# Linear attention and a gated causal unit on one core: nine tokens of a head per partition instead of four and a tail

## The chip, the core and the metric

The kernel runs on one core of a Trainium2 chip. The core has TensorE (PE), VectorE (DVE), ScalarE (ACT), GpSimd (POOL) and SyncE (SP); each takes its instructions in order from a list of its own and waits on semaphores for the others. Matrix products land in PSUM, which here is one tile `PS` of 128 partitions and 8 banks of 512 floats. Loads, stores and the transposing copies are DMAs, issued by SP, POOL or ACT.

The metric is the device time of one execution, in microseconds.

## The reference

There are 8 batches, 8 heads, 576 tokens, and 64 values per head. The first half is a linear attention with exponential features, the second a gate made by a causal convolution of five taps:

```python
def phi(x):
    proj = x @ w_phi                                  # 64 -> 128
    proj = proj - max(abs(proj), axis=-1)
    return concatenate([exp(proj), exp(-proj)])       # 256 features
kv = einsum('bhsf,bhsd->bhfd', phi(k), v)
z  = sum(phi(k), axis=2)
x  = (phi(q) @ kv) / (phi(q) @ z + 1e-06)             # heads side by side: 8 x 576 x 512
gate = 1 / (1 + exp(-sum_k conv_w[k] * x[s - 4 + k])) # zeros ahead of token 0
out  = (gate * (x @ w_val)) @ w_out
```

Inputs and output are float32; the kernel's matmuls take bf16.

## The kernel before, in words

A **unit** is two heads (a pair, `hp`) of one batch over the first 512 tokens. Each partition holds four consecutive tokens of a head, so a token is named by partition and place `j` (0 to 3). The last 64 tokens of two batches make a **tail** unit: 36 units in all, 32 mains and 4 tails.

Steps of a main unit, by the names in the list:

- `T`, `Tc` (L331, L224 or L222): eight transposes of 128x128 put k and q into one PSUM bank; one copy takes them to SBUF. Row half 0 then holds one place, row half 1 the next.
- `PK`, `PQA` (L342): the projections with tokens on the partitions, 64-row matmuls into two banks each. `mKa`, `mK`, `mQa`, `mQ` (L356): their largest absolute values, on DVE.
- `K0` to `K3` (L388): the exponentials of k, plus and minus, per bank, on ACT. The maximum of k is not subtracted; `E` (L382, two small exponentials) makes the factors and `V` (L408, L412, on POOL) multiplies them into v, with the factor itself as a 65th column.
- `PQ` (L466) projects q with features on the partitions; `SH` (L476) subtracts its maximum by a matmul with a negative identity; `Qa`, `Q` (L484) are its four exponentials.
- `KV` (L445, L450): the sums over tokens, 4 results of four matmuls over 128 partitions and one from the tail (`VZ`, which has zeros where the other batch sits). `KVM` copies the result to SBUF as `KVS`.
- `NUM` (L509, tails L523), `XN` (L534, L536: reciprocal and product on DVE), `XP` (L545, L548): numerators, division, and a transposing DMA on SP into `XT` (mains) or `XH` (tails), channels on the partitions.

For a batch: `GA` (L604) does the five taps by 64x64 diagonal tiles, two blocks of 32 matmuls; `TH` (L612) a tanh of the halved sum (weights are halved, so that 0.5 * (tanh + 1) is the sigmoid); `VA` (L617) the value product; `GV` (L633) their product; `OUT` (L642), `OE` (L649, L651: times 0.5) and `ST` the output. Tails have `GAt` (L673, L681), `THt`, `GVt`, `OUTt` (L704), `OEt`, `STt` of their own. `HL` copies the four tokens in front of a tail.

Loads `LD` go through POOL's queue, those of the first v and the first pair of k through SP. The order of all the work is the string `ORDER`, written out in advance: one token a step, with the PSUM bank behind `@` and the engine behind `:`. Each engine executes its own instructions in this order; nothing is moved at run time.

Of the kernel before, what the change touches and what calls it, by code (L numbers as in the profile page):

```python
# [10 lines left out]
ALU = mybir.AluOpType  # L11
# [9 lines left out]
SM = 512  # L21
ST = S - SM
E1 = D + 1
PL = 144
TL = 80
NG = B // 2
NU = 9 * NG


# [3 lines left out]
LD7 LD6 CK0 CQ0 T1@1 LD2 ND0:A W20 Tc1:D PK1@2,5 mKa1 PQA1@6,1 K01 mK1 mQa1 mQ1 T0@0 LD0 Tc0:A  # L33
PQ1@3,4 PK0@7,6 K11 K21 mKa0 T2@0 E1 Tc2:D K31 K00 SH1 Qa1 LD1 PK2@1,0 mK0 mKa2 LD3 mK2 PQA2@3,5
mQa2 ZV0:P LD8 K20 mQ2 T3@2 E0 Tc3:D PQA0@3,5 mQa0 mQ0 K02 K10 K30 E2 K22 PK3@7,6 mKa3 PQA3@2,5
LD4 mQa3 Q1 LD9 PQ2@3,4 SH2 LD10 mK3 K32 K12 T4@0 Tc4:D PK4@1,0 K03 Qa2 mQ3 V0:P K23 V1:P KV1@3 Q2
LD5 V2:P mKa4 K33 K04 KVM1:D NUM1@4 PQ3@6,3 SH3 mK4 XN1 LD11 K13 KV2@2 K24 LD31 PQA4@7,4 KVM2:D E3
mQa4 K14 mQ4 PQ0@1,5 K34 SH0 LD30 Qa3 Qa0 NUM2@6 PQ4@2,0 T5@4 T6@1 Q3 SH4 Q0 XN2 Qa4 E4 Tc5:D
Tc6:D PK5@7,6 mKa5 K05 PQA5@3,1 PK6@2,5 mQa5 Q4 LD13 K15 mK5 LD12 V3:P K25 KV3@3 mQ5 V4:P mKa6 K06
LC0 K35 KVM3:D E5 V5:P LD32 LD39 PQ5@0,1 TP0@7 mK6 Vb0:P NUM3@3 CW0 XP1 XN3 K16 XP2 T7@7 Tc7:D K26  # L40
SH5 Qa5 PQA6@6,2 mQa6 PK7@3,7 mKa7 KV4@4 PQA7@6,0 mQ6 mQa7 XP3 K36 T8@5 Tc8:D mK7 PQ6@2,6 Q5
KVM4:A SH6 K07 NUM4@4 mQ7 XN4 E6 PK8@0,1 K17 mKa8 Qa6 K27 T9@2 Tc9:D Q6 XP4 PQA8@3,5 V6:P PQ7@4,6
SH7 mQa8 LD15 mK8 K08 K37 PQA9@2,3 mQ8 mQa9 KV5@7 KVM5:D mQ9 T10@5 Tc10:D K18 PQ8@0,2 SH8 Qa7
PK9@4,7 mKa9 T11@3 E7 V7:P Q7 PK10@5,6 Tc11:D K28 mKa10 LD14 DG0:P Qa8 K38 KV6@3 Q8 K09 NUM5@0 mK9
KVM6:D NUM6@2 XN5 K010 mK10 KV7@0 K29 K110 XN6 K19 KVM7:D T12@5 PK11@1,4 mKa11 K210 HL0:P Tc12:D
XP6 LD16 K39 GA0@2 K310 mK11 K011 NUM7@6 VAa1@0 LD40 XN7 E8 VAb1 TH0 GV1 V8:P PK12@2,5 PQA10@3,6
K111 PQ9@1,7 SH9 VAa2@0 K211 mQa10 mKa12 LD19 VAa0@3 mK12 E9 LD17 K311 Qa9 VAb0 mQ10 KV8@4 KVM8:D
VAb2 GV0 PQA11@1,6 K012 V9:P Q9 mQa11 K212 PQ10@4,7 SH10 mQ11 K112 T13@3 Tc13:D NUM8@1 XN8 E10
K312 Qa10 Q10 GA1@5 TH1 PK13@3,4 mKa13 NUM0@1 V10:P KV10@7 XN0 KVM10:D XP5 XP0 XP8 E11 E12 K013
mK13 VAa3@5 GV2 PQ11@6,1 SH11 K113 Qa11 V11:P VAb3 GV3 LD18 K213 NUM10@2 XN10 T14@0 Tc14:D Q11  # L50
KV11@7 XP7 PQA12@5,6 K313 GA2@2 E13 TH2 PK14@0,1 mQa12 mQ12 PQA14@4,5 OUT1@6 OE1:A KVM11:D
PQA13@7,2 mQa14 V12:P V13:P mKa14 LD34 K014 mQ14 mQa13 K114 PQ12@3,4 SH12 XP10 KV12@6 mQ13 T15@5
Qa12 KVM12:A Tc15:D OUT2@7 Q12 mK14 K214 NUM11@2 E14 PQ13@0,6 SH13 Qa13 XN11 XP11 NUM12@4 OE2:D
XN12 T16@2 VAa6@3 PK15@7,0 mKa15 GA3@4 mK15 K314 V14:P VAa4@1 Q13 Tc16:D VAb4 K015 TH3 PQA15@6,2
GV4 K215 K315 PQ14@5,4 SH14 mQa15 K115 mQ15 VAa5@1 VAb5 PK16@0,6 Qa14 VAb6 Q14 KV13@7 GV5 mKa16
mK16 Vb9:P K016 VAa7@2 T17@1 GV6 E15 V15:P Tc17:D LD33 KVM13:A KV14@5 LD22 HL1:P NUM13@3 K116 K216
PQ15@0,7 KVM14:A VAb7 XN13 K316 SH15 GV7 PK17@1,3 mKa17 Qa15 K017 Q15 K117 LD35 mK17 XP13
PQA16@5,6 mQa16 OUT3@4 XP12 K217 OE3:D mQ16 OUT0@2 OUT5@0 K317 OE5:A E16 V16:P OE0:D NUM14@4 T18@1
XN14 Tc18:D GAt0@6 THt0 ST1 GVt0 E17 PQ16@2,3 PK18@1,0 SH16 Qa16 mKa18 Q16 T19@4 Tc19:D GA4@5 TH4
PQA18@7,2 mK18 mQa18 E18 KV15@4 KVM15:D K018 LD38 K118 V17:P K218 OUT6@3 mQ18 OE6:D PQA17@7,6 K318  # L60
mQa17 mQ17 LD20 GA5@4 TH5 PK19@2,3 mKa19 PQ18@1,7 SH18 K019 KV16@0 mK19 Qa18 KVM16:D K119 E19
NUM15@5 VAa9@4 VAb9 LD21 V19:P K219 ST3 XN15 XP15 GV9 NUM16@0 XN16 Q18 LD24 T20@2 VAa8@5 XP16 VAb8
K319 T21@6 PQA19@4,0 PQ17@1,7 Tc20:D PK20@2,3 Tc21:A SH17 GV8 Qa17 mQa19 VAa10@5 VAb10 mKa20 K020
XP14 KV17@6 V18:P mQ19 Q17 GV10 VAa11@0 PK21@1,4 KVM17:D K120 mK20 mKa21 mK21 K220 VAb11 GV11
NUM17@5 XN17 OUTt0@2 K021 K221 LD26 KV19@7 OUT7@0 K320 OEt0:D OE7:D K121 T22@3 PQA20@5,2 mQa20
PQ19@1,6 mQ20 SH19 KVM19:A K321 Tc22:A HL2:A PK22@0,5 mKa22 NUM9@3 XN9 XP9 Qa19 OUT4@7 Q19 K022
# [12 lines left out]
XN25 HL4:A OUTt1@2 Q26 K028 K128 KVM26:D OUT14@7 OE14:D XP25 K228 PQA27@3,4 mQa27 mQ27 GA8@0 TH8
VAa16@7 VAb16 K328 OEt1:A NUM26@4 XN26 T29@3 Tc29:A NUM18@0 XN18 XP18 E28 OUT12@6 V28:P PK29@3,2  # L80
GV16 OE12:A PQ27@5,4 mKa29 PQA28@0,1 mQa28 mQ28 K029 SH27 Qa27 GA9@6 TH9 T30@0 ST11 VAa18@1 mK29
VAb18 Tc30:D PK30@0,5 GV18 V27:P OUT15@6 VAa17@7 VAb17 mKa30 Q27 OE15:D mK30 K129 E29 PQA29@4,6
V29:P mQa29 GV17 mQ29 PQ28@1,3 K229 K030 K130 SH28 T31@0 Tc31:D K230 VAa19@4 VAb19 Qa28 KV28@7 ST9
XP26 K329 PQA30@6,1 PQ29@2,0 SH29 GV19 mQa30 mQ30 Q28 KVM28:A K330 NUM28@3 XN28 PQ30@7,6 Qa29 E30
V30:P PK31@5,1 mKa31 SH30 PQA31@4,3 Q29 Qa30 mQa31 mK31 E31 mQ31 KV29@2 V31:P K031 K231 T32@0
OUT17@4 Tc32:D K131 OUT16@7 Q30 PK32@0,3 KVM29:D OE17:D KV30@2 mKa32 K331 OE16:A NUM29@4 KVM30:D
K032 T33@6 XP28 mK32 XN29 XP29 GA10@1 LD29 K132 Tc33:D PQA32@4,5 K232 K332 E32 PQ31@7,0 mQa32
HL5:P TH10 mQ32 OUT19@6 OE19:A NUM30@3 XN30 XP30 KV31@5 KVM31:A SH31 Qa31 Q31 PQA33@1,6 PK33@2,3
ST15 mKa33 mQa33 mQ33 GA11@4 VAa20@7 TH11 VAb20 VAa22@1 mK33 V32:P VAb22 T34@6 PQ32@4,5 K033 SH32
E33 GV22 Tc34:D NUM31@0 VAa21@6 VAb21 GV20 K133 XN31 V33:P PK34@2,7 K233 K333 mKa34 Qa32 Q32 mK34  # L90
# [10 lines left out]
"""


class _U:
    pass

@with_exitstack
def kernel(  # L110
# [11 lines left out]
    nc = tc.nc  # L122
    ctx.enter_context(nc.allow_low_precision("bf16 operands of the matmuls"))

    const = ctx.enter_context(tc.tile_pool(name="const", bufs=1))
    loadp = ctx.enter_context(tc.tile_pool(name="loadp", bufs=3))
    loadv = ctx.enter_context(tc.tile_pool(name="loadv", bufs=3))
    tailp = ctx.enter_context(tc.tile_pool(name="tailp", bufs=2))
# [635 lines left out]
```

## Time and profile before

| | |
|---|---|
| median of three runs | 234.17 us (233.95 to 235.0) |
| span of the profiled execution, first to last instruction | 232.5 us |
| its own time | not given apart from its span; the three runs stand 1.5 to 2.5 us above it |
| busy: PE, DVE, ACT, POOL | 205.8, 184.2, 188.6, 125.4 us |
| mean granted TensorE clock | 0.972 |
| DMA | 30.90 MB in 62002 packets |

Matmuls are pipelined: the time a row gives for one is its latency, and a block's length is the distance between the starts of two blocks. Engines are called busy when any of their instructions runs. The clock column gives the share of full speed that TensorE was granted. In the chain of waits each piece starts where what released it ended.

### The profile page before, as it was taken

The page shows a single profiled execution, that of the slowest core. Times are in us where ns is not written, and L with a number is a line of the kernel's source. Part 1 is how long each engine was busy: PE and PEld are TensorE (multiplying, and loading weights), DVE is VectorE, ACT ScalarE, POOL GpSimd, SP SyncE. Part 2 cuts the span into 40 slices and gives each one's busy share as a digit, 9 for nine tenths or more (in the row PEclk, how much of TensorE's full clock was granted, in tenths as well). Part 3 has the DMA queues.
Part 4 walks back from the last instruction along what each step waited for, and adds up shares of the span by engine and source line. Part 5 has one row for each costly group of instructions (what it writes and reads, how often), then busy time and mean ns, then how long its engine had stood idle before and what let it go on. Part 6 is the DMA issues. An engine that isn't in the chain of part 4 may idle for free.

```text
span 232.5 us, 8372 instructions
## 1 busy us (share of the span) xinstructions
PE 205.8 (89%) x3497; PEld 139.5 (60%) x3516; DVE 184.2 (79%) x335; ACT 188.6 (81%) x419; POOL 125.4 (54%) x142
## 2 busy tenths in 40 slices
PE   1286797888999989899999999999899999999991
PEld 1264675666666746567666766766476667564550
DVE  5559669999989979699999879897799788554451
ACT  3189869999997988599999979998899999934251
POOL 8909935999979437774919751564526241100000
PEclk9998579999999999999999999999999999999997
DMA  8997995979999942999994992499903928126195
GB/s 151 246 198 97 106 180 80 92 101 178 129 194 128 139 32 32 129 257 177 128 114 68 180 186 92 39 115 126 214 6 37 169 77 259 38 52 200 27 355 185
DMA packets 62002, 30.90 MB, mean 133 GB/s; under 512 B 33420, under 2 KB 59148, under 8 KB 61964
## 3 DMA queue, kind: packets, MB, share of 16 engines
q0 software_dynamic: 36144, 14.29, 58.2%
q1 hardware_dynamic: 25468, 15.78, 33.6%
q8 instruction: 27, 0.44, 0.8%
q10 hardware_dynamic: 352, 0.30, 0.4%
q14 instruction: 11, 0.09, 0.2%
HBM read 30.48 MB, written 9.44 MB: 172 GB/s over the span
## 4 chain that ended last, share of the span: by engine, by line
PE 69%; ACT 11%; DMA 9%; DVE 5%; issue 3%; SPq 1%; POOL 1%; POOLq 0%; DVEq 0%; ACTq 0%
PE PS L617 11%; PE PS L642 10%; PE PS L342 7%; PE PS L604 7%; PE PS L476 7%; PE PS L445 6%; PE PS L331 6%; DMA XT<-XN 6%; PE PS L509 5%; ACT QTIL L484 5%; ACT KTIL L388 3%; DMA kT<-in_k_dram 3%; PE PS L466 3%; PE PS L681 2%; DVE MQ L356 2%
## 5 line engine op out<-in xcount | busy, mean ns | idle before, releaser
L408 POOL TENSOR_TENSOR VT<-vN,E 128x1024 bf16<-128x1024 bf16 x27 | 51.5, 1907 | 60.4 <-issue 34.2
L388 ACT ACTIVATE KTIL<-PS 128x512 bf16<-128x512 f32 x128 | 76.7, 666 | 5.3 <-DVE MK L356 5.1
L484 ACT ACTIVATE QTIL<-PS 128x512 bf16<-128x512 f32 x128 | 71.0, 666 | 2.5 <-PE PS L476 1.1
L356 DVE TENSOR_REDUCE MK<-PS 128x4 f32<-128x512 f32 x72 | 47.9, 683 | 7.5 <-PE PS L342 7.2
L356 DVE TENSOR_REDUCE MQ<-PS 128x4 bf16<-128x512 f32 x72 | 47.4, 683 | 1.3 <-PE PS L342 1.2
L342 PE MATMUL PS<-W,T 64*128 64x128 bf16 x576 | 29.6, 227 | 5.8 <-DVE T L224 1.9
L617 PE MATMUL PS<-XT,WVAL 128*128 128x512 bf16 x128 | 33.8, 380 | 0.3 <-DMA XT<-XN 0.3
L342 PEld LDWEIGHTS <-T 64*128 64x128 bf16 x576 | 18.3, 98 | 21.8 <-issue 11.9
L642 PE MATMUL PS<-WOUT,GV 128*128 128x512 bf16 x111 | 29.9, 380 | 1.2 <-issue 0.5
L633 DVE SCALAR_TENSOR_TENSOR GV<-GATE,PS 128x512 bf16<-128x512 bf16 x32 | 21.6, 681 | 5.9 <-ACT GATE L612 3.1
L445 PE MATMUL PS<-VT,KTIL 128*128 128x65 bf16 x512 | 25.4, 198 | 0.8 <-DVE T L224 0.6
L536 DVE TENSOR_TENSOR XN<-PS,RCP 128x512 bf16<-128x512 f32 x36 | 24.9, 691 | 1.2
L445 PEld LDWEIGHTS <-KTIL 128*128 128x128 bf16 x512 | 22.8, 100 | 3.7 <-DVE T L224 0.8
L476 PE MATMUL PS<-nident,MQ 128*128 128x128 bf16 x288 | 23.9, 229 | 0.5 <-issue 0.5
L612 ACT ACTIVATE GATE<-PS 128x1024 bf16<-128x1024 f32 x16 | 16.7, 1044 | 8.8 <-PE PS L604 8.7
L476 PEld LDWEIGHTS <-MQ 128*128 128x128 bf16 x288 | 17.6, 102 | 9.5 <-issue 8.8
L224 DVE COPY T<-PS 128x1024 bf16<-128x1024 bf16 x31 | 21.1, 684 | 2.7 <-PE PS L331 2.3
L509 PEld LDWEIGHTS <-QTIL 128*128 128x128 bf16 x512 | 19.3, 99 | 5.5 <-DVE KVS L224 1.1
L509 PE MATMUL PS<-KVS,QTIL 128*128 128x65 bf16 x512 | 21.4, 196 | 1.3 <-DVE KVS L224 0.8
L450 PE MATMUL PS<-VZ,KTt 128*128 128x65 bf16 x128 | 21.9, 196 | 0.0
L604 PE MATMUL PS<-XT,DIAG 64*64 64x384 bf16 (+3 forms) x512 | 20.6, 299 | 1.0 <-issue 0.8
L642 PEld LDWEIGHTS <-GV 128*128 128x128 bf16 x128 | 11.3, 98 | 12.4 <-issue 0.6
(73 smaller groups left out, 304.1 us busy)
## 6 DMA issues: line engine op xcount, KB each, us to landing
out_dram<-OS SPq DMA_DIRECT2D x14, 512.0 KB, 3.8
kN<-in_k_dram POOLq DMA_DIRECT2D x7, 512.0 KB, 9.0
qN<-in_q_dram POOLq DMA_DIRECT2D x7, 512.0 KB, 8.4
vN<-in_v_dram POOLq DMA_DIRECT2D x7, 512.0 KB, 6.9
vF<-in_v_dram SPq DMA_DIRECT2D x2, 512.0 KB, 7.6
out_dram<-OSt SPq DMA_DIRECT2D x8, 128.0 KB, 2.4
out_dram<-OS SPq DMA_DIRECT2D x4, 256.0 KB, 2.9
qT<-in_q_dram POOLq DMA_DIRECT2D x8, 64.0 KB, 5.2
```

Source lines behind the costliest of these rows:

```text
L342: nc.tensor.matmul(PS[:, bank[rg], blk * P:(blk + 1) * P], u.T[r, i, blk, :], W2[r, :], start=True, stop=True,)
L356: nc.vector.tensor_reduce(dst, PS[:, bank, :].rearrange("p (b f) -> p b f", f=F), AX.X, ALU.max, apply_absolute_value=True,)
L388: nc.scalar.activation(u.KT[:, ft, rg, :, :].rearrange("p b f -> p (b f)"), PS[:, u.PK[rg], :], AF.Exp, scale=1.0 if ft == 0 else -1.0,)
L408: eng.tensor_tensor(dst[:, :, :, 0:D], x.unsqueeze(1).to_broadcast([n, 2, 8, D]), e.unsqueeze(3).to_broadcast([n, 2, 8, D]), ALU.mult,)
L445: nc.tensor.matmul(o, u.KT[:, ft, rg, h2 * 2 + j2, :], u.VT[:, ft, (h2 * 2 + j2) * 2 + rg, :], start=(c == 0), stop=False,)
L476: nc.tensor.matmul(PS[:, u.PQ[rg], blk * P:(blk + 1) * P], u.MQ[:, rg, blk:blk + 1].to_broadcast([P, P]), nident[:, :], start=False, stop= ...
L484: nc.scalar.activation(u.QT[:, ft, rg, :, :].rearrange("p b t -> p (b t)"), PS[:, u.PQ[rg], :], AF.Exp, scale=1.0 if ft == 0 else -1.0,)
L509: nc.tensor.matmul(ps[:, j2, x * E1:(x + 1) * E1], u.QT[:, ft, rg, h2 * 2 + j2, :], u.KVS[:, (ft * 2 + h2) * E1:(ft * 2 + h2 + 1) * E1], s ...
L536: nc.vector.tensor_tensor(u.XN[:, :, :, :], nv[:, :, :, 0:D], RCP[:, :, :].unsqueeze(3).to_broadcast([P, 2, 4, D]), ALU.mult,)
L604: nc.tensor.matmul(ps[c, par, j0 * P:j1 * P], DIAG[r, dt, 4 - dl, :], mv, start=(i == 0), stop=(i == len(parts) - 1), skip_group_check=True,)
L617: nc.tensor.matmul(PS[:, m.val[jt], :], WVAL[:, dt, jt * P:(jt + 1) * P], XTs[m.b % 2][:, dt, :, 16:PL], start=(dt == 0), stop=(dt == 3),)
L642: nc.tensor.matmul(PS[:, bank[0], :], m.GV[:, jt, j * P:(j + 1) * P], WOUT[:, jt, :], start=(jt == 0), stop=(jt == 3),)
```

## The change

Each partition now holds nine consecutive tokens of a head: 64 partitions per head, two heads to a tile of 128, tokens `9r + j`. Every batch is on its own. A main unit (32 of them) has the places 0 to 7 of a head pair. Place 8 of all eight heads of a batch is a **head group** `h` (8 of them), which takes the part of the tails, with steps `hT`, `hPK`, `hPA`, `hSH`, `hKp`, `hV`, `hNUM`, `hXP`, `hGA`, `hVA`, `hOUT` and so on.

- Loads are whole tensors of a batch, 2304 contiguous bytes per partition and head pair; there are no tail loads.
- `T` transposes each head's 64 partitions apart: 16 matmuls of 64 rows and 64 columns, into two banks.
- `KV` sums over 64 rows per head, the two heads in two banks; the ninth step of each sum is the head group's.
- The maximum of k is negated on POOL (`NG`), so that one ACT instruction (`E`) makes both factors.
- `XT` holds 13 slots of 64 columns: slots 4 to 12 are the places 0 to 8, slots 0 to 3 the tokens that come before place 0, copied one column to the right from slots 9 to 12 (`HL`, on POOL). Every tap is then a contiguous run of 512 columns.
- `GA` uses 32x32 diagonal tiles: 4 row groups to 4 column groups, four banks, 80 matmuls a batch. Output channels come out permuted in groups of 32, so the columns of `w_val` and the rows of `w_out` are permuted to match (`WVX` by copies, `WOX` by DMAs).
- The last four mains and the last head group go through TensorE (`XQ`, `hXQ`) and a copy (`XC`, `hXC`) instead of the transposing DMA; the last batch's taps, tanh, values and outputs are cut finer (`Ga`, `Gb`, `Th`, `VAc`, `VAd`, `OUa`, `OUb`, `SO`).
- Ten matmuls on zeros (`Z`) stand among the first steps.
- `ORDER` is new throughout. Stores are cut by place: two per `ST`, 64 partitions each.

```diff
-PL = 144
-TL = 80
-NG = B // 2
-NU = 9 * NG
+J = 9
+NP = 4
+R = 64
...
 ORDER = """
-LD7 LD6 CK0 CQ0 T1@1 LD2 ND0:A W20 Tc1:D PK1@2,5 mKa1 PQA1@6,1 K01 mK1 mQa1 mQ1 T0@0 LD0 Tc0:A
...
+XZ1:D Z1@0 Z1@1 Lk11:P CQ0 IF0:D Lv13:S ND0:D CK0 Z1@2 LC0 Lq11:P Z1@3 Lk12:P Tk0@4,5 Lq12:P W0 Tkc0:D
+Tq0@6,7 Tqc0:D PK0@0,1 XZ0:D T1@2,3 mKa0 Lq1:P Lk1:P Kc0 PQ0@4,5 Tc1:D PA0@6,7 LV0 Kd0 mKb0 Kb0 Lv12:S
...
+    def rows(name, b, p0, p1):
+        return src[name][b, 2 * p0:2 * p1].rearrange("(n h) (r j) d -> (h r) n (j d)", h=2, j=J)
...
+    def op_Z(n, bank):
+        for _ in range(n):
+            nc.tensor.matmul(PS[:, bank[0], :], zt[:, 0:P], zt[:, :], start=True, stop=True)
...
+    def op_LX(jt, eng):
+        c = 64 if jt == 2 else 32
+        for p0 in range(0, P, c):
+            p1 = p0 ^ (32 * jt)
+            engines[eng].dma_start(WOX[p0:p0 + c, jt - 1, :], WOR[p1:p1 + c, jt, :])
...
     def op_T(i, bank):
-        for n, name in enumerate(("k", "q")):
-            for blk in range(4):
-                nc.tensor.transpose(u.Tps[:, n, blk, :], col(u, name, blk), ident_bf[:, :])
+                    for h in range(2):
+                        r = slice(h * 64, h * 64 + 64)
+                        o = PS[:, bank[h], 0:256].bitcast(BF16)
+                        nc.tensor.transpose(
+                            o[:, (n * 4 + x) * R:(n * 4 + x + 1) * R], t[r, u.hp, cols], ident_bf[r, r],
+                        )
...
+    def op_NG(i, eng):
+        MK = units[i].MK
+        engines[eng].tensor_scalar_mul(MK[:, 1, :, :], MK[:, 0, :, :], -1.0)
     def op_E(i):
-        for ft in range(2):
-            nc.scalar.activation(
-                u.E[:, ft, :, :].rearrange("p b r -> p r b"), u.MK[:, :, :],
-                AF.Exp, scale=-1.0 if ft == 0 else 1.0,
-            )
+        nc.scalar.activation(
+            u.E[:, :, :].rearrange("p f (x a) -> p f a x", a=2), u.MK[:, :, :, :], AF.Exp, scale=-1.0,
+        )
...
     def op_KV(i, bank):
-                for c in range(4):
-                    nc.tensor.matmul(
-                        o, u.KT[:, ft, rg, h2 * 2 + j2, :],
-                        u.VT[:, ft, (h2 * 2 + j2) * 2 + rg, :],
-                        start=(c == 0), stop=False,
-                    )
-                nc.tensor.matmul(
-                    o, ut.KT[:, ft, h2, u.hp, :],
-                    VZ[u.G % 2][u.b % 2][:, ft, 2 * u.hp + h2, :],
-                    start=False, stop=True,
-                )
+        for ft in range(2):
+            for c in range(9):
+                for h in range(2):
+                    r = slice(h * 64, h * 64 + 64)
+                    if c < 8:
+                        w = u.KT[r, ft, c // 4, (c % 4) * F:(c % 4 + 1) * F]
+                        x = u.VT[r, ft, c % 4 * 2 + c // 4, :]
+                    else:
+                        w, x = m.KT[r, ft, u.hp * F:(u.hp + 1) * F], m.VT[r, ft, u.hp, :]
+                    nc.tensor.matmul(
+                        PS[:, bank[h], ft * E1:(ft + 1) * E1], w, x, start=(c == 0), stop=(c == 8),
+                    )
...
+    def op_XQ(i, bank):
+        u.XP = PS[:, bank[0], 0:256].bitcast(BF16)
+        xf = u.XN[:, :, :, :].rearrange("p a y d -> p (a y d)")
+        for x in range(4):
+            nc.tensor.transpose(u.XP[:, x * P:(x + 1) * P], xf[:, x * P:(x + 1) * P], ident_bf[:, :])
...
+    def halo(eng, b, p0, p1, j0, j1):
+        x = XTs[b % 2][:, p0:p1, :].rearrange("p a (s r) -> p a s r", r=R)
+        copy(eng, x[:, :, j0 - 5:j1 - 5, 1:R], x[:, :, j0 + 4:j1 + 4, 0:R - 1])
...
-    def op_GA(n, bank):
-        for i, (dl, j0, j1) in enumerate(parts):
-            for dt, r, c, par in quarters(q2):
-                nc.tensor.matmul(
-                    ps[c, par, j0 * P:j1 * P], DIAG[r, dt, 4 - dl, :], mv,
-                    start=(i == 0), stop=(i == len(parts) - 1), skip_group_check=True,
-                )
+    def op_GA(b, bank, dts=(0, 1, 2, 3)):
+        for tap in range(5):
+            for dt in dts:
+                for i in range(4):
+                    o = (i ^ dt) * 32
+                    c = (i ^ dt) % 2 * 32
+                    r = slice(i * 32, i * 32 + 32)
+                    nc.tensor.matmul(
+                        PS[o:o + 32, m.gate[dt], :], DIAG[r, dt, tap, c:c + 32],
+                        XT[r, dt, tap * R:(tap + 8) * R],
+                        start=(tap == 0), stop=(tap == 4), skip_group_check=True,
+                    )
...
+    def op_hGA(b, bank):
+        for y in range(2):
+            for tap in range(5):
+                for z in range(2):
+                    dt = 2 * z + y
+                    for i in range(2):
+                        r = slice(i * 64, i * 64 + 64)
+                        o = (i ^ z) * 64
+                        nc.tensor.matmul(
+                            PS[o:o + 64, bank[z], y * R:(y + 1) * R], DIAG[r, dt, tap, :],
+                            XT[r, dt, (8 + tap) * R:(9 + tap) * R],
+                            start=(tap == 0), stop=(tap == 4), skip_group_check=True,
+                        )
...
+    def store(eng, m, x, n):
+        ov = out[m.b].rearrange("(r j) o -> r j o", j=J)
+        for jj in range(2):
+            j = 2 * x + jj
+            eng.dma_start(
+                ov[:, j:j + 2 * n - 1:2, :],
+                m.OS[x // 2][jj * 64:jj * 64 + 64, x % 2:x % 2 + n, :],
+            )
```

The other steps of the head groups (`hPK`, `hSH`, `hKp`, `hNUM`, `hVA`, `hOUT`) are those of a main on half the columns: `hNUM` and `hOUT` write 64 partitions each way, and `hVA` streams 64 columns.

More of the change, by code (lines that the diff above doesn't have):

```diff
@@ L37 @@
[L37 to L42, printed above, removed]
@@ new lines, in hqexp, with op_hQp, op_hQm, op_hNUM @@
+    def hqexp(m, ft):
+        if not hasattr(m, "QT"):
+            m.QT = pools["hQT"].tile([P, 2, 2, 2 * P], BF16, name="hQT")
+        nc.scalar.activation(
+            m.QT[:, ft, :, :], banks(m.PQ)[:, :, 0:256], AF.Exp, scale=1.0 if ft == 0 else -1.0,
+        )
+    def op_hQp(b):
+        hqexp(batches[b], 0)
+    def op_hQm(b):
+        hqexp(batches[b], 1)
+    def op_hNUM(b, bank):
+        m = batches[b]
+        m.NUM = bank
+        for z in range(2):
+            for h in range(2):
+                for ft in range(2):
+                    for x in range(2):
+                        y = z * 2 + h
@@ new lines, in op_hXQ, with op_hXC @@
+    def op_hXQ(b, bank):
+        m = batches[b]
+        m.XP = PS[:, bank[0], 0:P].bitcast(BF16)
+        for z in range(2):
+            nc.tensor.transpose(
+                m.XP[:, z * P:(z + 1) * P],
+                m.XN[:, 0, 2 * z:2 * z + 2, :].rearrange("p y d -> p (y d)"), ident_bf[:, :],
+            )
+    def op_hXC(b, eng):
+        m = batches[b]
+        copy(
+            eng, XTs[b % 2][:, :, 12 * R:13 * R].rearrange("p (x z) r -> p z x r", x=2),
+            m.XP.rearrange("p (z x r) -> p z x r", z=2, x=2),
+        )
@@ L653, in op_OE @@
     def op_OE(n, eng):
[L654 to L677 removed]
+        m, x = batches[n // 4], n % 4
@@ new lines, in op_OE, with op_ST @@
+        if x // 2 not in m.OS:
+            m.OS[x // 2] = pools["OS"].tile([P, 2, DM], FP32, name="OS")
+        half(eng, m.OS[x // 2][:, x % 2, :], PS[:, m.out[x], :])
+    def store(eng, m, x, n):
+        ov = out[m.b].rearrange("(r j) o -> r j o", j=J)
+        for jj in range(2):
+            j = 2 * x + jj
+            eng.dma_start(
+                ov[:, j:j + 2 * n - 1:2, :],
+                m.OS[x // 2][jj * 64:jj * 64 + 64, x % 2:x % 2 + n, :],
+            )
+    def op_ST(n, eng):
+        store(engines[eng], batches[n // 2], 2 * (n % 2), 2)
@@ L718, with op_hOE, op_hST @@
+    def op_hOE(b, eng):
+        m = batches[b]
+        m.hOS = pools["hOS"].tile([P, 256], FP32, name="hOS")
+        half(eng, m.hOS[:, :], PS[:, m.hout, 0:256])
+    def op_hST(b, eng):
+        m = batches[b]
+        ov = out[b].rearrange("(r j) o -> r j o", j=J)
+        for x in range(2):
+            engines[eng].dma_start(
+                ov[:, 8, x * 256:x * 256 + 256], m.hOS[x * 64:x * 64 + 64, :],
+            )
     ops = {n[3:]: f for n, f in locals().items() if n.startswith("op_")}
```

934 lines of the change are left out of this document (525 added, 409 removed), and 14 rows, old and new, of the table LOADS.

## The prediction

> **What bounds it.** I read the page's first two parts, then the busy time by stage, with the stages cut at the end of the clock dip (32.3 us) and after the last feature exponential (204.4 us), then the chain of waits for the price of each TensorE block.
>
> ```profile
> span 232.5 us, 8372 instructions
> PE 205.8 (89%) x3497; PEld 139.5 (60%) x3516; DVE 184.2 (79%) x335; ACT 188.6 (81%) x419; POOL 125.4 (54%) x142
> PEclk9998579999999999999999999999999999999997
> ```
> ```profile
> 0.00:12.00 12.00, 2.85 (x32) 2.23 (x32) 6.25 (x12) 2.71 (x4) 10.16 (x18) 1.00 1.08 199
> 12.00:22.00 10.00, 7.68 (x88) 5.27 (x86) 7.53 (x13) 9.70 (x24) 4.73 (x5) 0.98 1.20 164
> 22.00:32.30 10.30, 8.85 (x118) 7.07 (x115) 6.14 (x11) 7.54 (x17) 8.81 (x11) 0.52 1.12 117
> 32.30:204.40 172.10, 163.73 (x2972) 112.69 (x2984) 152.16 (x277) 160.02 (x364) 101.74 (x109) 1.00 0.96 121
> 204.40:232.50 28.10, 22.66 (x303) 12.26 (x303) 12.08 (x23) 8.61 (x13) 0.00 (x0) 0.95 0.54 169
> ```
>
> The columns are the stretch, its length, and busy us of PE, PE's weight loads, DVE, ACT and POOL, then the granted clock. In the long middle PE is busy 163.73 of 172.10 (95%) and ACT 160.02 (93%): two bounds almost level, with 8.4 us of PE idle. The rest of PE's 26.7 us idle is 9.15 in the first 12 us, 3.8 up to 32.3, and 5.4 behind the last exponential, where PE works nearly alone. In the third stretch the granted clock is 0.52, so its 8.85 us of PE work would be about 4.6 at full clock.
>
> The span is 232.5; the runs' median is 234.17, so I add 1.7 us to a predicted span.
>
> **TensorE, block by block.** Prices from the chain of waits (start, us, what); the group of KV sums by its window.
>
> ```profile
> 117.97 0.22 PE PS L476 x4
> 118.61 0.63 PE PS L523 x32
> 125.12 0.45 PE PS L331 x8
> 128.82 0.49 PE PS L509 x16
> 129.31 1.22 PE PS L604 x32
> 135.77 0.86 PE PS L617 x4
> 148.45 0.70 PE PS L673 x40
> 149.15 1.00 PE PS L681 x16
> 159.68 0.59 PE PS L642 x2
> 160.28 0.33 PE PS L342 x8
> 160.60 0.22 PE PS L466 x2
> 160.82 0.22 PE PS L342 x8
> ```
> ```profile
> 101.14:101.78 0.64, 0.64 (x25) 1.00 1.05 411
> ```
>
> Two blocks of L342 cost 0.33 and 0.22: the first follows L642's full-height tiles, the second another 64-row block. A change of tile shape thus costs about 0.1 us, and I take 0.1 off the blocks that begin with one (L523 0.53, L604 1.12, L673 0.60, L681 0.90).
>
> Transposes. Before, 8 of 128 rows cost 0.45 a unit. After, 16 of 64 rows with 64 columns, two row halves side by side. No row has this shape. Floor: L523, 32 matmuls of 65 columns in column halves, 16.5 ns each. Ceiling: L342, the same 64x128 weights with 128 columns, 27.5 ns. I take 18, near L523, whose streamed length is the same: 16 x 18 = 0.29, so -0.16 x 32 units = -5.1 us; ends -6.0 (16.5 ns) and -0.3.
>
> KV sums. Before, 20 full-height matmuls in 0.64. After, 36 of 64 rows, weights 64x128, 65 columns: the same two bounds give 0.59 to 0.99; at 18 ns 0.65, so +0.3; ends -1.6 and +11.2.
>
> Taps. Before, two blocks of 32 a batch, 16 x 1.12 = 17.9 us. L604 streams 10240 columns over four 64x64 tiles in 1.12 us, 9.1 columns per ns, while one full-height stream (L617, 2048 columns in 0.86) gives 2.4: the quarters nearly all run at once. After, 80 of 512 columns in 16 tiles of 32x32: 40960 columns a batch. All sixteen at once need 1.1 us; L673 shows 15 ns a matmul, which gives 1.2; eight at once, 2.1. I take 1.2: 8 x 1.2 = 9.6, -8.3; ends -9.3 and -1.1.
>
> Tails. Before, per pair of batches: T 0.45, projections 0.44, PQ 0.22, shift 0.45, numerators 0.53, taps 0.60, value 0.90, output 0.86, that is 4.45 x 4 = 17.8 us. After, per batch, by halves of the same rows: T 0.22, projections 0.22, PQ 0.11, shift 0.22, numerators 0.27, 40 taps of 64 columns 0.6 (15 ns; 0.3 if a half-length stream halves it), value 16 x 32 ns 0.51 by L509's 31 ns, output 0.44: 2.6 x 8 = 20.8, +3.0.
>
> Added: 18 transposes of 128 columns for the last heads (L331's 56 ns), +1.0; 10 matmuls on zeros at L617's 215 ns, +2.2; tile shapes change 179 times instead of 165 in TensorE's list, +1.4. Value and output products of the mains, projections, PQ, shift and numerators keep count and length.
>
> Sum: -5.1 + 0.3 - 8.3 + 3.0 + 1.0 + 2.2 + 1.4 = -5.5 us, with ends -12 (every floor, the short head taps at 0.3) and +17 (every ceiling at once).
>
> **The other engines.**
>
> ```profile
> L484 ACT ACTIVATE QTIL<-PS 128x512 bf16<-128x512 f32 x128 | 71.0, 666 | 2.5 <-PE PS L476 1.1 <-ACT KTIL L388 1.0
> L382 ACT ACTIVATE E<-MK 128x8 f32<-128x8 f32 x72 | 12.6, 266 | 0.1
> L222 ACT ACTIVATE T<-PS 128x1024 bf16<-128x1024 bf16 x5 | 5.2, 1033 | 3.7 <-PE PS L331 3.6
> L222 ACT ACTIVATE KVS<-PS 128x260 bf16<-128x260 f32 x10 | 4.3, 427 | 1.3 <-PE PS L450 1.2
> L224 DVE COPY T<-PS 128x1024 bf16<-128x1024 bf16 x31 | 21.1, 684 | 2.7 <-PE PS L331 2.3 <-ACT KTIL L388 0.3
> L224 DVE CAST KVS<-PS 128x260 bf16<-128x260 f32 x22 | 9.3, 424 | 2.8 <-PE PS L450 2.5
> L408 POOL TENSOR_TENSOR VT<-vN,E 128x1024 bf16<-128x1024 bf16 x27 | 51.5, 1907 | 60.4 <-issue 34.2 <-ACT E L382 18.7 <-DMA vN<-in_v_dram 7.1
> L412 POOL CAST VT<-E 128x16 bf16<-128x16 f32 x31 | 7.9, 256 | 0.0
> ```
>
> ACT gets no relief. The 288 exponentials of 512 columns stay. E falls from 72 to 40 (-32 x 0.175 = -5.6), T copies from 5 to 3 (-2.1), KVS copies rise from 10 to 24 (+6.0), and narrow copies and gates of the heads add about 2: near 189 us. DVE loses 14 KVS copies (-5.9), a memset pair and one VT, and gains narrow copies of the heads: about -5. Its T copy now writes runs of 64 in a pattern with a bank step; if that lost the rate of 1024 elements in 684 ns, each of 30 would cost up to 0.5 more. I price it at nothing because the innermost run stays dense; at 15 us DVE would come to 194, above ACT.
>
> POOL: 32 V of 1.9 us, 8 of half width for VZ's 8 of full, 40 new negations (at most 0.25 by the 16-wide cast, 10 us), a halo copy of 1008 elements a batch instead of 16 (at most the V's 1.9, 13 us), six weight copies: about 135 to 140, with some 85 idle. The negation puts POOL between DVE's row maximum and ACT's E; behind it in that queue stand V and load issues.
>
> ```profile
> 3.83 7.29 DMA kT<-in_k_dram
> 208.91 3.52 DMA XT<-XN
> ```
> ```profile
> 226.65 1.11 SPq L716 DMA_DIRECT2D out_dram<-OSt  x2
> 216.64 2.90 SPq L548 DMA_TRANSPOSE XH<-XN  x2
> ```
>
> SP: 40 transposing DMAs become 42, stores 26 become 52, and 10 short weight moves come in: 42 x 1.45 + 62 x 0.55 = 95 us of issue, below the span but in line, so a store in front of a transpose delays it 0.55. Loads lose the separate tails that PE waits for at 3.83 to 11.25, and carry 12% more bytes per pair. Unit 1 needs its own two loads, issued first on POOL, so I count 8 us of PE idle there for 9.15, with 7 and 11 as ends.
>
> **The end.** After the last exponential, PE's list still holds five output blocks (4.3), 10 value matmuls (2.15), the taps of batch 7 (1.2), two heads' taps and values (2.2), three head outputs (1.3), the last numerators and transposes (0.4) and ten shape changes (1.0): 12.6 us, for 22.7 before. The wait for the transpose at 208.91 is gone (0.11 of TensorE and a copy instead), but NUM, XN, transpose, copy, halo and taps follow each other. PE idle there: 6.5 for 5.4, the difference being two more store issues. That work is moved in front of the last exponential, not removed; it is in PE's sum already.
>
> **Sum.** PE busy 205.8 - 5.5 = 200.3, less 1.5, a third of what the slow-clock stretch can give back (0 to 4.3; the zero matmuls keep PE occupied but loads pace the start). Idle: 8 + 3.8 + 8.4 + 6.5 = 26.7. Span 198.8 + 26.7 = 225.5, time 227.2. By ACT: 189 less the 7 it has after its last exponential, plus 23 idle before it (9.3 at the start less one, 14.7 later), is 205; with an end of 20 us, 225. The two agree, so I take 227.
>
> **Rivals.** (a) 64-row tiles run no faster than L342, 27.5 ns. Transposes and KV together then cost 4.8 + 10.9 = 15.7 us more than I took: PE +10, span 241, time 243, slower. With 52 such matmuls in each of 32 units, it turns at about 22 ns. For: L342 is their weight shape. Against: its 27.5 is just 128 columns over two tiles. Chance 0.10.
>
> [...] L523 at 16.5 and L673 at 15 ns speak against it; chance 0.03. [...]
>
> [...] Chance 0.02. [...]
>
> (c) POOL's negation waits behind a V (1.9 us) and ACT, in order, stands at E. Each such stall is up to 1.9 us; 40 units times 0.2 us average cancels the gain, and 0.4 makes it 235. For: ACT already feeds POOL late (18.7 us of POOL idle behind E). Against: POOL is over a third idle, and exponentials of the same unit stand ahead of E. Chance 0.06.
>
> (d) The new list leaves PE and ACT fitting less well: PE's middle at 92% instead of 95% costs 6 us, time 233 to 234, about no change. Four-bank taps and two-bank transposes and KV sums speak for it; DVE's lighter load against. Chance 0.12.
>
> (e) All goes well: PE -12, clock dip gone (-4), shorter end (-2): time 214 to 217. Chance 0.17.
>
> The forecast, 227 with its own range 221 to 232, has 0.50.
>
> **How the numbers follow.** Differences within 0.5% (233.0 to 235.3) can't be told from no change. Faster: forecast 0.48, (e) 0.17, a third of (d) 0.04: 0.69. Same: 0.01 and 0.04 of the same two, 0.05. Slower: (a), (b1), (b2) 0.15, (c) 0.06, the rest of (d) and the forecast 0.05: 0.26. The range, 213 to 244, takes in (a), (c) and (d) at their worked times and leaves out (b1), (b2), the fast edge of (e) and the slow edges of (a) and (c), less than 0.2 together.
>
> **What would show it.** Right: 16 transposes in about 0.3 us and 36 KV matmuls in 0.65 with starts under 20 ns; 80 taps in 1.2; PE busy near 200 and ACT near 189; the last exponential near 205 and the end 20 us behind it. [...]

## The result, and the profile after

The changed kernel takes 324.05 us (median of four runs, 322.7 to 325.38) where the kernel before took 234.58 beside it: a ratio of 1.382, 95% interval 1.376 to 1.388. One of the four runs of the kernel before took 332.91 us and stands apart; the other three took 233.95 to 235.0. The forecast was 227 with a range of 213 to 244, so the change is far slower than any case that was priced. Parts 1 and 2 of the changed kernel's page show what sort of miss it is:

```profile
span 321.6 us, 10938 instructions
PE 233.4 (73%) x4752; PEld 148.9 (46%) x4752; DVE 184.2 (57%) x341; ACT 197.0 (61%) x406; POOL 118.0 (37%) x176
PEclk9997957798589789997669999855999679999998
```

DVE and ACT are busy about as long as was forecast (179 and 189). No engine has grown into a bound; every one of them now stands still for a quarter of the span or more. By stage, cut at the end of the start and at the last feature exponentials (columns as in the prediction):

```profile
0.00:12.00 12.00, 6.00 (x71) 3.11 (x71) 5.20 (x14) 4.91 (x8) 6.50 (x15) 1.00 0.91 219
12.00:32.00 20.00, 16.96 (x301) 11.99 (x301) 14.89 (x27) 16.17 (x36) 15.09 (x24) 0.91 1.22 208
32.00:294.00 262.00, 192.38 (x4079) 124.21 (x4072) 156.12 (x284) 166.20 (x347) 95.10 (x134) 0.85 0.48 82
294.00:321.60 27.60, 18.05 (x317) 9.60 (x315) 8.02 (x17) 9.73 (x19) 1.31 (x4) 0.96 0.37 92
```

The start is better than forecast and the end within 4 us of it. The middle, 172 us before, is 262, with TensorE idle for 69.6 us of it (8.4 before) and ACT for 95.8, at a granted clock of 0.85.

The priced blocks are not to blame. Three of them in the timeline and in the chain of waits of the changed kernel (start, us, what):

```profile
64.43 0.29 PE L336 MATMUL PS<-ident_bf,kN 64*128 64x64 bf16 x8
...
64.55 0.28 PE L336 MATMUL PS<-ident_bf,qN 64*128 64x64 bf16 x8
...
64.67 0.39 PE L372 MATMUL PS<-W,T 64*128 64x128 bf16 x8
```
```profile
116.23 0.57 PE PS L506 x36
...
181.55 1.30 PE PS L814 x80
```

From the first transpose at 64.43 to the next block at 64.67, sixteen transposes take 0.24 us (0.29 forecast); 36 matmuls of the KV sums take 0.57 (0.65) and 80 taps 1.30 (1.2). These are blocks that nothing stopped; others in the same chain take longer, KV sums up to 1.17.

What engines wait for is odd, though. The same timeline a little later, with the idle time and its releaser in brackets:

```profile
65.17 0.21 DVE L610 RECIPROCAL RCP<-PS 128x8 f32<-128x8 f32 x1 [1.83 <-PE PS L372]
65.41 0.69 DVE L611 TENSOR_TENSOR XN<-PS,RCP 128x512 bf16<-128x512 f32 x1
...
66.15 0.59 PE L846 MATMUL PS<-XT,WVX 128*128 128x512 bf16 x2 [1.10 <-DVE XN L611]
...
66.22 1.57 ACT L457 ACTIVATE KT<-PS 128x512 bf16<-128x512 f32 x3 [2.37 <-DVE XN L611]
```

By the list this is `NUM5@0,7 T10@3,4 Qa6 PK9@2,6 XN5 Kd9 Kc9 VAb1`. The division of unit 5 (`XN5`) reads banks 0 and 7. It waits for the projections `PK9`, which write banks 2 and 6. Behind it the exponentials `Kd9`, which read bank 6, and the value product `VAb1`, in bank 5 since `VAa1@5`, wait for it in turn. None of them shares a bank or a byte with it.

That is theory F, formed from these lines: `banks(a)` names two banks as one strided range, `PS[:, a0:a1+1:a1-a0]`, and the semaphore waits are placed as if such an access touched every bank between its two. `XN5` then counts as a user of all eight. In the list of the changed kernel 101 of the 144 two-bank groups are not neighbours; they skip 267 banks in all. In its instructions, 243 of the 1305 waits on a semaphore of a compute engine join two accesses that share no bank, and only lie within each other's span. The kernel before names its banks `b:b+2`, and has none among 1228. Two rivals: L, the new list fits the engines badly whatever the banks (rival (d) of the prediction, enlarged), and R, banks are given out again too soon.

### The profile page after: what moved, and what is told of

It reads as the page before. It is cut to its first block, busy times and chain, and to the rows that moved or that the text cites. A ratio compares the mean times of both kernels' runs of the same rounds, so it can differ in the third digit from the quotient of the medians.

```text
span 321.6 us, 10938 instructions
## 1 busy us (share of the span) xinstructions
PE 233.4 (73%) x4752; PEld 148.9 (46%) x4752; DVE 184.2 (57%) x341; ACT 197.0 (61%) x406; POOL 118.0 (37%) x176
## 4 chain that ended last, share of the span: by engine, by line
PE 35%; ACT 16%; DVE 12%; issue 3%; DMA 1%; SPq 0%; DVEq 0%; ACTq 0%
PE PS L846 7%; ACT QT L573 6%; PE PS L882 6%; PE PS L814 4%; ACT KT L457 4%; PE PS L372 3%; PE PS L506 3%; PE PS L600 3%; DVE XN L611 3%; DVE T L212 3%; PE PS L529 3%; ACT GATE L824 2%; PE PS L520 2%; PE PS L968 1%; DVE MQ L387 1%
## 5 line engine op out<-in xcount | busy, mean ns | idle before, releaser
L573 ACT ACTIVATE QT<-PS 128x512 bf16<-128x512 f32 x128 | 68.8, 610 | 29.8 <-PE PS L529 19.5
L457 ACT ACTIVATE KT<-PS 128x512 bf16<-128x512 f32 x128 | 71.1, 610 | 22.2 <-PE PS L372 8.9
L212 DVE COPY T<-PS 128x1024 bf16<-128x1024 bf16 (+1 forms) x30 | 20.0, 671 | 26.8 <-ACT QT L573 5.3
L506 PE MATMUL PS<-VT,KT 64*128 64x65 bf16 x1024 | 26.3, 205 | 12.5 <-DVE T L212 4.9
L846 PE MATMUL PS<-XT,WVX 128*128 128x512 bf16 x96 | 29.3, 410 | 3.9 <-DVE XN L611 2.7
L506 PEld LDWEIGHTS <-KT 64*128 64x128 bf16 x1024 | 23.3, 104 | 16.0 <-DVE T L212 5.1
L882 PE MATMUL PS<-WOX,GV 128*128 128x512 bf16 x96 | 27.1, 389 | 1.0 <-DVE GV L872 0.5
L600 PE MATMUL PS<-KVS,QT 128*128 128x65 bf16 x512 | 23.5, 199 | 5.1 <-DVE hMK L387 1.5
L600 PEld LDWEIGHTS <-QT 128*128 128x128 bf16 x512 | 21.0, 102 | 9.0 <-issue 6.4
L520 PE MATMUL PS<-T,W 64*128 64x512 bf16 x64 | 15.9, 449 | 10.6 <-DVE T L212 4.2
## 6 DMA issues: line engine op xcount, KB each, us to landing
qN<-in_q_dram POOLq DMA_DIRECT2D x7, 576.0 KB, 10.2
```

The costliest lines, as they stand in the source:

```text
L212: engines[eng].tensor_copy(dst, x)
L457: nc.scalar.activation(o, x, AF.Exp, scale=1.0 if ft == 0 else -1.0)
L506: nc.tensor.matmul(PS[:, bank[h], ft * E1:(ft + 1) * E1], w, x, start=(c == 0), stop=(c == 8),)
L573: nc.scalar.activation(o, x, AF.Exp, scale=1.0 if ft == 0 else -1.0)
L600: nc.tensor.matmul(PS[:, bank[x // 2], y * E1:(y + 1) * E1], u.QT[:, ft, h * 4 + x, :, :].rearrange("p j r -> p (j r)"), u.KVS[:, h, ft * ...
L846: nc.tensor.matmul(PS[:, m.val[jt], :], wval(dt, jt), XTs[m.b % 2][:, dt, 4 * R:12 * R], start=(dt == 0), stop=(dt == 3),)
```

## Experiments on the banks

**The same list with other bank numbers.** In `narrow` and `wide` the eight banks are renamed throughout `ORDER`; which step shares a bank with which, and when, stays exactly as it was. Only the distance within the pairs changes: 185 skipped banks and 394 for 267.

```diff
-NUM4@3,6 ... VAa1@5 ... NUM5@0,7 ... PK9@2,6
+NUM4@1,4 ... VAa1@5 ... NUM5@2,7 ... PK9@3,1     # narrow
+NUM4@2,7 ... VAa1@3 ... NUM5@4,6 ... PK9@0,2     # wide
```

> The changed kernel with its eight banks renamed, one fixed permutation: order of steps and order of reuse stay exactly as they are; the banks skipped inside two-bank accesses fall from 267 to 185 in sum, and waits on an instruction of no common bank from 243 to 177. Theory F, with the 97 us of excess spread over the 267: 227 + 185 x 0.36 = 294 us (280 to 308). Rivals L and R: 324 us, since nothing they look at changes.

> The same with the permutation that makes the gaps widest: 394 banks skipped for 267, 304 waits on an instruction of no common bank. Theory F: 227 + 394 x 0.36 = 370 us (340 to 390; it saturates where the waits already stand in line). Rivals L and R: 324 us.

`narrow` took 298.31 us (two runs, 295.36 and 301.25), `wide` 365.96 (365.47 to 366.46; ratio 1.565, 1.554 to 1.575). Between 185, 267 and 394 skipped banks the time goes 298, 324, 366: about 0.31 and 0.33 us for each bank (0.35 for the first by the faster run of `narrow`). Neither L nor R can move the time here, since the steps, their order and the sharing are the same. Both fall for this part. Nor is the access itself slower for reaching farther: the division `XN` takes 691 ns in the kernel before, with neighbours, and 691 in the changed kernel and in `wide`, with banks up to seven apart.

**Only neighbours.** `adj` keeps the order of the steps and places every two-bank group anew, on neighbouring banks.

```diff
-NUM4@3,6 ... VAa1@5 ... NUM5@0,7 ... PK9@2,6
+NUM4@6,7 ... VAa1@5 ... NUM5@0,1 ... PK9@6,7
```

> Only the bank numbers in the list change: the same steps in the same order, but every two-bank access now reads neighbouring banks (144 of 144, where 43 were before). Theory F (a two-bank access with a gap is ordered against every bank between its two; 243 of 1305 waits on another engine name an instruction that shares no bank with the waiter): no such wait is left, and the kernel comes to the 227 us that the engines' work gave, 215 to 240. Rival L (the new list fits the engines badly, whatever the banks): 324 us as now. Rival R (banks are used again too soon): this list uses banks again a little later than the old one by a decaying count of steps (898 for 935), so 4% of the excess goes: 320 us.

It took 252.03 us (249.41 to 254.37; ratio 1.081, 1.072 to 1.090). No wait of that kind is left in it. So 72 of the 90 us lost go with the spans, and 18 stay, 25 above the forecast.

**The other way round.** `spread` is the kernel before with its banks renamed so that neighbours come to stand three or five apart; its order and sharing stay too.

```diff
+    MAP = [0, 3, 6, 1, 4, 7, 2, 5]
+    def pair(b):
+        a = sorted((MAP[b], MAP[b + 1]))
+        return PS[:, a[0]:a[1] + 1:a[1] - a[0], :]
...
-        ps = PS[:, bank[0]:bank[0] + 2, :]
+        ps = pair(bank[0])
```

> The kernel before, with its banks renamed (0 to 7 become 0, 3, 6, 1, 4, 7, 2, 5), so that its 56 two-bank groups (numerators, taps) lie three or five banks apart; nothing else changes, and 113 waits on an instruction of no common bank arise where there were none. Theory F: 56 groups with 2 to 4 skipped banks, 134 in sum, x 0.36 = 48 us: 282 us (255 to 300). Rivals L and R: 234 us.

It took 290.99 us (290.93 to 291.06; ratio 1.244, 1.236 to 1.252). Parts 1 and 2 of its page:

```profile
span 289.1 us, 8364 instructions
PE 221.1 (76%) x3497; PEld 148.7 (51%) x3516; DVE 187.9 (65%) x335; ACT 191.8 (66%) x419; POOL 125.6 (43%) x142
```

The work is that of the kernel before (DVE 184.2, ACT 188.6) and the span 57 us longer, 0.43 us for each of 134 skipped banks: the loss can be put into the tuned kernel by renaming its banks alone.

**The spans taken away, the banks left.** `split` is the changed kernel with its own bank numbers. Each access to two banks that are not neighbours becomes two accesses to one bank each.

```diff
+    def parts(a):
+        if abs(a[1] - a[0]) == 1:
+            return [(slice(0, 2), banks(a))]
+        return [(slice(x, x + 1), PS[:, a[x]:a[x] + 1, :]) for x in range(2)]
...
-        copy(eng, u.KVS[:, :, :], banks(u.KVb)[:, :, 0:2 * E1])
+        for w, a in parts(u.KVb):
+            copy(eng, u.KVS[:, w, :], a[:, :, 0:2 * E1])
```

> The changed kernel with its own banks; each access of DVE and ACT to two banks that are not neighbours (101 of 144 groups) becomes two accesses to one bank each, so no access spans banks that it does not use. ACT and DVE get some 6 to 8 us more of fixed cost. Theory F (two-bank accesses were ordered against the banks between): the 97 us excess is gone but for a few us, and banks come free as the list was written for. Theory P (what remained in the run with neighbouring banks came from re-placed banks coming free too late): 232 to 246. Theory D (it came from the list and from stalls that no bank causes): 250 to 262, the run with neighbours plus the added work.

It took 235.32 us (233.42 to 237.84; ratio 1.008, 1.004 to 1.013). Its page, the stage of the middle, and the longest pieces of its chain of waits in which TensorE waited for nothing that the profile shows:

```profile
span 233.0 us, 11139 instructions
PE 201.4 (86%) x4752; PEld 131.9 (57%) x4752; DVE 187.1 (80%) x431; ACT 193.9 (83%) x464; POOL 117.8 (51%) x176
```
```profile
32.00:212.00 180.00, 164.12 (x4018) 109.38 (x4015) 156.11 (x359) 161.90 (x396) 93.93 (x132) 0.99 0.72 120
```
```profile
44.95 2.21 issue
...
92.58 1.73 issue
...
100.65 1.22 issue
```

With no access spanning a bank it does not use, 89 of the 97 us over the forecast are gone, though DVE has 90 instructions more (a division of 512 columns in one access took 691 ns, each of the two of 256 columns 424). The order of steps is the same in `adj`, so the 17 us that it takes beyond this belong to its placement, or to the shorter accesses of `split`. By their lists of waits TensorE waits 14.0 us in all for ACT in `adj` and 1.0 in `split`, over half of it in blocks that read nothing ACT made, such as transposes (L335), projections (L371) and values (L845): they wait for a bank that ACT still reads. For this placement R is the likely reason, which the count of 898 for 935 in the expectation did not show; it was not tested apart. For the change itself R falls. The granted clock returned by itself: 0.99 in the middle for 0.85, and TensorE's busy time fell by 32 us for the same matmuls.

## Experiments on the 8 us that were left

**Loads.** In `split` and `adj` TensorE stops within blocks, as in the three rows above: after 23 of 36 matmuls of a KV block, after 7 of the 16 head values that follow 40 small taps, after 15 of 16 transposes. It takes 9504 instructions, weight loads counted, for 7013 before. Theory I: its own instructions come late while loads fill the DMA queues. `once` is `adj` without the loads of batches 2 to 7.

```diff
     def tensor(name, b):
+        b = min(b, 1)
...
     def load(name, b, p0, p1, eng):
+        if b > 1:
+            return
```

> The kernel with neighbouring banks (adj), with the loads of k, q and v of batches 2 to 7 left out: these batches use the tensors of batch 1 again, so their results are not the reference's; everything else is the same. It takes some 20 MB off the DMA queues after the first 40 us. Theory I (TensorE stands still within blocks, 2.51 us at 47.7, 2.57 at 84.4, 1.26 at 140.9 in the chain of waits of adj, because its own instructions arrive late behind the loads, and its clock dips after such a stop): these gaps are gone, the clock holds from 60 us on, 240 (236 to 245). Theory D (the list fits TensorE and ACT badly, loads or not): 249 to 253, gaps or not.

241.92 us (241.35 to 242.15; ratio 1.035, 1.031 to 1.038): 10 us less than `adj`, and one stop near 1 us (0.99 at 133.11) instead of three over 1 us. The granted clock, 0.77 from 45 to 60 us and 0.89 from 75 to 90 in `adj`, where the two longest of these stops stand, is 1.00 in both stretches of `once`. `splitonce` does the same to `split`, and so takes both causes away:

> The split kernel with the loads of batches 2 to 7 left out, as in once: these batches use the tensors of batch 1 again, so their results are not the reference's; all other work is the same. It removes both suspected causes at once: accesses that span banks they do not use, and TensorE's stops within blocks (together 8 us in the chain of split) that came and went with the loads. If these two make up the difference from the forecast: no stop over 1 us in the chain, PE busy near 200 with 26 to 28 idle, 225 to 229. If loads cost nothing in split, where TensorE is busier: 233 to 237.

227.63 us (224.15 to 228.7), where the kernel before took 233.44. Its page and its middle:

```profile
span 225.5 us, 11128 instructions
PE 204.4 (91%) x4752; PEld 134.6 (60%) x4752; DVE 185.8 (82%) x431; ACT 192.5 (85%) x464; POOL 103.8 (46%) x158
```
```profile
32.00:204.00 172.00, 165.25 (x4086) 110.68 (x4086) 157.04 (x366) 162.69 (x402) 83.85 (x120) 1.00 0.38 70
```

No stop in its chain is over 0.7 us, and its middle has 6.75 us of TensorE idle where the forecast had 8.4. The span is the 225.5 of the forecast. Whether the kernel before pays for its loads as well was the control, the same edit in `beforeonce`:

> The kernel before with the loads of batches 2 to 7 (and of the tails after the first) left out; these batches use the tensors of batch 1 again, so their results are not the reference's. It is the other half of the comparison with splitonce, where leaving out the loads was worth about 8 us. If late instructions and late transposes behind loads are a cost of the change (TensorE runs 35% more instructions): before gains at most 2 us, 231.5 to 234. If the loads cost both kernels alike: 225 to 229, and the change has then gained nothing at all.

230.29 us (228.9 to 231.03; ratio 0.984, 0.975 to 0.993): 3.4 us less than the 233.72 beside it, between the ranges of the two expectations. So both kernels pay, the changed one (7.7 us, from 235.32 to 227.63) about twice as much; the interval of the smaller figure, 1.7 to 5.8 us, leaves 2 to 6 us to the change, if 7.7 is taken as it stands.

Where the stops fall shows that they are late instructions. Instructions come by DMA, in a queue of their own (packets, MB, share of the 16 engines; first in `split`, then in the kernel before):

```profile
q8 instruction: 37, 0.61, 1.0%
...
q8 instruction: 27, 0.44, 0.8%
```

That is one packet of some 16 KB for 257 of TensorE's 9504 instructions, and for 260 of its 7013. The stops in the chain of `split` at 44.95, 80.48, 92.58, 100.65 and 143.81 come behind 1473, 3009, 3521, 3777 and 5825 instructions in TensorE's records, whole multiples of 256 apart, and TensorE goes on 1.4 to 2.8 us after a packet of this queue has landed. Nine stops at such places take 8.4 us in `split`; one of 0.7 is left in `splitonce`. Loads delay other DMAs too: the transposing DMAs into `XT` land after 4.0 us (median; at most 12.6) in `split` and after 3.1 (at most 5.2) in `splitonce`.

**Loads set apart.** `even` is `split` with the same loads, moved so that none follows closely on another.

```diff
-Ka0 PA1@0,1 ... Lk2:P mQa1 ... LO0
+Ka0 PA1@0,1 ... mQa1 ... LO0          # Lk2 stands 70 steps later, and so on for 18 loads
```

> The split kernel with the loads of batches 2 to 7 moved in the list so that they stand about evenly (before, several follow each other from 12 to 34 us and from 72 to 91 us); banks and all other steps as in split. Theory I (stops of TensorE within blocks, 2.21 us at 44.95, 1.73 at 92.58 and 1.22 at 100.65 in the chain of split, together 8 us, come from its own instructions arriving late behind loads): the long stops go or shrink, 226 to 231. If the loads are not what the stops depend on: 234 to 237, stops as long as before elsewhere.

Its runs lie far apart (237.17 to 248.93, median 246.56), so only this is read from them: not one is as fast as the median of `split`. That fewer loads at a time make shorter stops is not borne out: the longest in its trace is 2.97 us, for 2.21 in `split`. What about a load makes an instruction packet late stays open, since the profile does not show when a packet was asked for.

**Other orders.** If only the list is bad, another list should win. Four were made from `split`, without a step added or removed, two-bank groups put on neighbours (132 to 138 of 144) and the rest split.

```diff
-Tq0@6,7 Tqc0:D PK0@0,1 XZ0:D T1@2,3 mKa0 Lq1:P Lk1:P Kc0 PQ0@4,5 Tc1:D PA0@6,7 LV0 Kd0 mKb0 Kb0
+Tkc0:D Tq0@2,3 Tqc0:D PK0@0,1 Kd0 mKb0 Ka0 Kb0 Z1@2 mKa0 PA0@2,3 NG0:P E0 Lv12:S T1@4,5 Tc1:D     # relist1
+Tkc0:D Tq0@2,3 Tqc0:D Lv12:S TP0@7 Z1@6 Lq1:P CW0 PK0@0,1 Kd0 mKa0 Lk1:P LV0 Lk2:P mKb0 Kb0       # order1
```

> The split kernel with its steps put in another order and its banks chosen anew (no step added or removed; two-bank accesses on neighbours where that costs no wait, split elsewhere; loads spread out). Theory F and D together (what is left of the loss is the order of steps, not the work): TensorE's middle is over 93% busy, 216 to 226, faster than the kernel before. If the work itself sets the time (more instructions, changes of tile shape, late instructions of TensorE): 230 to 238.

> A second order of the same steps, found independently of relist1; the same expectations: 216 to 226 if the order of steps is what is left, 230 to 238 if the work itself sets the time. If only one of the two is fast, the gain is luck of one order and not of the kind.

262.37 us (261.38 to 265.26; ratio 1.123, 1.114 to 1.132) and 260.55 (259.61 to 261.48; ratio 1.113, 1.106 to 1.120): a clear miss. Both were made with their loads spread out too, and `even`, where that is the only change, is slower than `split`. The waits of `relist1` (engine and line, what it waited for, us in total, times, longest):

```profile
ACT KT L467 <- DVE MK L397: 18.1, 20, 2.6
...
DVE MK L397 <- ACT KT L467: 14.9, 17, 2.0
```

An exponential on ACT and a row maximum on DVE both read one bank here (`Kd0 mKb0`, `Ka0 Kb0 ... mKa0`). They take turns, 33 us of waits in all, and 34 in `relist3`. In `split` this pair costs 0.6 us. Its list crosses them (`mKa0 ... Kc0`, then `mKb0 Kb0`): one engine is in one bank while the other is in the next. `order1` and `order2` are meant to respect that too.

> A third order of the same steps, with banks chosen anew and 137 of the 144 two-bank groups on neighbours, the other 7 split. What the two orders before it had lost (20 waits of ACT's k exponentials on DVE's row maxima of the same bank, 18.1 us, and 17 the other way, 14.9 us) is respected: in this order ACT and DVE are meant to read different banks at the same time. Theory G (an order of steps has to respect two things that take turns: the span of a two-bank access, and two engines reading one bank): 220 to 231, faster than the kernel before. If only the first of the two matters, this order gains nothing over the other two: 255 to 265. If the work itself (9500 instructions of TensorE, its stops) sets the time: 233 to 240, as split.

> A fourth order, found independently of order1 under the same two rules, with 132 of 144 groups on neighbours: 220 to 231 by theory G, 255 to 265 if only the span of two-bank accesses matters, 233 to 240 if the work itself sets the time.

247.03 us (243.75 to 251.03; ratio 1.043, 1.032 to 1.054) and 254.95 (250.08 to 256.98; ratio 1.074, 1.060 to 1.088). The turns between these two are down to 1.7 and 0.6 us in all, and both lists are still slower than `split`. A stretch of the chain of `order2`:

```profile
95.41 0.19 POOL VT L493
95.61 6.71 issue
...
102.44 1.04 POOL XT L221
...
103.52 0.90 PE PS L832 x46
104.42 2.24 issue
```

POOL stands for 6.71 us ahead of the halo copy, which TensorE's taps need: the transposing DMA issued at 92.07 lands 10.2 us later, just as the copy begins (the median of these DMAs is 4.8). The taps then stop after 46 of 80 for 2.24, with an instruction packet in flight from 104.28 to 105.16. These lists were ordered by the durations of the engines alone, and neither delay was in them; whether that is all that they lost is not shown. No version here beats the kernel before with all of its work done; `split` comes nearest, 0.8% behind.

## Why the prediction was wrong

**The step that failed** is the sum's "Idle: 8 + 3.8 + 8.4 + 6.5 = 26.7", in its third term: 8.4 us for the middle, carried over from the kernel before. It measured 69.6. The list of the change was taken to keep the engines as busy as the old one had, with 6 us for rival (d) if it did not. What stands in its place is a cost for each two-bank access by the banks that it skips. `narrow`, `wide`, `spread` and `split` show it: 0.3 to 0.4 us a bank, 89 us together with the lower clock (0.85 in the middle for 0.99).

**Rival (d)** had the place right: "Four-bank taps and two-bank transposes and KV sums speak for it". Its size was wrong by fifteen times, since it thought of banks in use and not of banks between. The numbers that give it away, 101 of 144 pairs apart, stood in the list before any run.

**Blocks**: right. Transposes 0.24 for 0.29, KV 0.57 for 0.65, taps 1.30 for 1.2. TensorE's 200.3 is 201.4 in `split`, its 233.4 in the changed kernel the same matmuls at a lower clock. Rival (a) is refuted by the same rows: 15 to 16 ns a matmul, below 18 and below the floor of 16.5 that was allowed for. What (b1) and (b2) were given their 0.03 and 0.02 for, no run shows: matmuls started every 15 to 16 ns, and the 80 taps took 1.30 us.

**ACT, DVE, POOL.** ACT 197.0 for 189, and 192.6 in `adj`; DVE 184.2 for 179: its instructions add up to less than before (195.4 us for 199.2), but fewer of them overlap. POOL has 118.0 for 135 to 140: issuing loads of k, q and v takes it 19.7 us for 38.1 before, which the working leaves out, and the halo copy was priced at its upper end (1.9 us; it takes 1.0). The two that could have hurt did not:

```profile
L212 DVE COPY T<-PS 128x1024 bf16<-128x1024 bf16 x28 | 19.3, 689 | 26.8 <-ACT QT L573 5.3 <-PE PS L600 4.3 <-PE PS L336 4.1
L428 POOL TENSOR_SCALAR MK<-MK 128x8 f32<-128x8 f32 x32 | 7.3, 231 | 75.2 <-DVE MK L387 75.2
```
```profile
ACT E L434 <- POOL MK L428: 2.9, 2, 1.8
```

The T copy, in runs of 64 with a bank step, keeps its rate (689 ns; 684 before), and ACT waits 2.9 us for the negation in the whole run, so rival (c) is out.

**Start and end.** TensorE is idle 6.0 of the first 12 us for 8. The 1.5 us that the sum took back from the slow clock were the author's estimate, and no run of the change is without the matmuls on zeros; the granted clock from 22.0 to 32.3 us is 0.83 for 0.52. The last feature exponential:

```profile
297.32 0.60 ACT L731 ACTIVATE hQT<-PS 128x512 bf16<-128x512 f32 x1 [1.62 <-PE PS L600]
```

From its end at 297.9 to 321.6 are 23.7 us, for 20. In `split` the same stretch is 20.9 (212.1 to 233.0), so the bank waits reach into it.

**The forecast as a sum** stood on the loads costing what they cost before. With spans and loads both taken away the span is 225.5, as forecast, but the forecast did not leave loads out: agreement there is luck, two errors of opposite sign. TensorE is busy 204.4 us of it for the 198.8 of the sum and idle 21.1 for 26.7, and `beforeonce` shows that the kernel before, from which the idle terms came, pays some 3 us for its loads too. With its loads and without the spans, the change is worth 0.8% more time, not 3% less.

## What to carry over

Where a kernel names several PSUM banks in one access, look at what the access spans and not only at what it reads: count the pairs that are not neighbours, and give pairs to neighbours or split the access where the list cannot (splitting was the cheaper here, 235 us against 252). An idle term may be carried from one order of work to another only after asking what each wait in the new order is placed against. And two engines that read one bank took turns here (33 us of waits in `relist1`, 0.6 in `split`, whose list crosses them), so an order should cross them.

## What the runs showed of the hardware

Matmuls of 64 rows and 64 or 65 columns, alternating between two row halves, started every 15 to 16 ns (16 in 0.24 us, 36 in 0.57), and 80 of 32x32 tiles with 512 columns took 1.30 us: 31 columns per ns, three times the 9.1 of the 64x64 tiles before. TensorE's instructions reached it in packets of 16 KB, one for 256 of them, and it stopped where one was late (8.4 us in `split`). That ACT and DVE do not read one bank together is the order that the waits make in these programs (33 us of waits in turns in `relist1`, 34 in `relist3`); no run here shows what would happen without it.
